# q and k of batches 2 to 7 transposed by DMA two batches ahead, those of batches 0 and 1 on the matrix engine

## The chip, the core and the metric

The kernel runs on one core of one Trainium2 chip. A core has five engines that each run their own list of instructions: PE (matrix multiply, with its weight loads shown apart as PEld), ACT (ScalarE), DVE (VectorE), POOL (GpSimd) and SP (SyncE). Here POOL issues all loads, and SP issues the stores of the output. Sixteen DMA engines carry what both issue. The metric is the device time of one execution in microseconds (us), lower is better.

## The reference

Eight batches of causal attention with a window of 128 and an ALiBi slope, eight heads of 64, 576 positions; the result is laid out as 4608 tokens of 512 and goes through two matrix products with h * cos(h) between them.

```python
scores = scale * np.matmul(q, k.transpose(0, 1, 3, 2))
bias = slopes[:, None, None] * (-np.abs(rel).astype(np.float32))[None, :, :]
mask = (rel >= 0) & (rel < window)
scores = np.where(mask, scores + bias[None], -1000000000.0)
attn = softmax(scores)                       # over the keys
attn_out = np.matmul(attn, v)
x = attn_out.transpose(0, 2, 1, 3).reshape(4608, 512)
h = x @ w_in                                 # 512 x 2048
out = (h * np.cos(h)) @ w_out                # 2048 x 512
```

Inputs and output are float32 in memory; the kernel computes in bf16 and accumulates in float32.

## The kernel before

Work is cut in two ways: attention goes by **batch** (8 of 576 tokens), the two matrix products go by **chunk** (9 of 512 tokens). The main loop runs over chunks c: `moe1(c)` (first product, line 596; for chunk 0 in halves, line 619; then the cosine on ACT, line 601, and the product on DVE, line 605), then `attention(c + 1)`, then `moe2(c)` (second product, line 642, whose result is copied to `ob` and stored by SP, line 654).

For the scores, q and k of a batch must lie with the head's 64 dimensions on the partitions. Before, `load_qk` (line 298) brings q and k into `qrows` and `krows` with the sequence on the partitions: eight DMAs per batch, issued by POOL. `qk_transposes` (line 375) then turns them over on PE. One call is a group of 18 transposes into two PSUM banks, followed by two copies (lines 386 on ACT, 387 on DVE, whichever is free) into `qt` and `kt`. A batch has four such calls (q and k, two halves each): 72 transposes and 8 copies. `qt` and `kt` exist once; `qrows` and `krows` too. In the loop they belong to batch c + 1 and stand between the moe1 matmuls of chunk c or in the last part of the attention before it.

Attention works in units of two heads and 256 queries, and a ninth unit for the last 64 queries of all heads ("t"). Each unit is a chain over engines: scores on PE (lines 414 and 424), exp on ACT (446, 454), mask on DVE (462, 469), probabilities times v on PE (490, 492, 504, 507), division on DVE (524 to 538), transposing back on PE (554, 568), and a copy into `xT` (582 on ACT, 583 on DVE).

PSUM has eight banks: `SB` 4 to 7 for scores, `UB` 2 and 3 for the attention output, `OB` 0 and 1 for moe2; moe1 borrows from UB and SB, and the q and k transposes from SB.

The order on each engine is written by a list scheduler inside the kernel (`Plan.schedule`): every operation has a planned occupation and latency and a priority, and the engine that can start first gets its best candidate. The result is a fixed list per engine. At run time an engine only waits on semaphores; if something is late, all that stands behind it on its engine waits too. POOL and SP kept program order before the change.

Of the kernel before, what the change touches and what calls it, by code (L numbers as in the profile page):

```python
# [13 lines left out]
NBLK = 5  # L14
# [20 lines left out]
class Plan:  # L35
# [3 lines left out]
    SWITCH = 95  # L39
    TABLE = 1330  # L40

    def __init__(self, nc, ctx):
# [44 lines left out]
    def schedule(self):  # L87
        free = {e: 0 for e in ENG}
        wire = 0
        mode, table = 0, None  # L90
# [18 lines left out]
        while avail:  # L109
# [130 lines left out]
def bass_alibi_sliding__then__act_gcu_kernel(  # L240
# [8 lines left out]
    with ExitStack() as ctx:  # L249
# [30 lines left out]

        ps = ctx.enter_context(nc.psum_tensor("ps", [128, 8, 512], F32))
        SB, UB, OB = [4, 5, 6, 7], [2, 3], [0, 1]

        slopes = [2.0 ** (-8.0 * (h + 1) / H) for h in range(H)]

        def keys_ap(x, pr, c):
            t = tr["k"][:, :].rearrange("p (k t) -> p k t", k=NPAIR)
            return t[64 * x:64 * x + 64, pr, 128 * c:128 * c + 128]

        def query_ap(x, pr, blk, width):  # L290
            t = tr["q"][:, :].rearrange("p (k t) -> p k t", k=NPAIR)
            return t[64 * x:64 * x + 64, pr, 128 * blk:128 * blk + width]


        def load_qk(which, src, b, pl):
            fns = []
            for g in range(2):
# [3 lines left out]
                        "h (s j) d -> s h (j d)", j=9)))  # L301
            op("pool", fns, w=[("qB", which, pl)], dma=f"ld{which}{pl}", occ=1250, lat=1250)

        def load_v(b, order=range(NBLK)):
            for t in order:
# [20 lines left out]
        def constants():  # L326
# [19 lines left out]
            op("dve", lambda e: e.memset(halfpi[:, :], math.pi / 2.0), w=["halfpi"])  # L346
            op("dve", lambda e: e.memset(
                tr["k"][:, :].rearrange("p (k t) -> p k t", k=NPAIR)[:, :, 576:640], 0.0),
               w=["ktail"])

# [12 lines left out]

        def qk_transposes(which, pl, banks):
            jj = ((0, 5), (5, 9))
# [15 lines left out]
            for n, (j0, j1) in enumerate(jj):  # L381
                o = tr[which][:, :].rearrange("p (g l t) -> p g l t", g=2, l=2)[
                    :, :, pl, 0:576].rearrange("p g (s j) -> p g s j", j=9)[:, :, :, j0:j1]
# [3 lines left out]
                    "dve": lambda e, o=o, i=i: e.tensor_copy(o, i)},  # L387
                   w=[("B", banks[n]), ("tr", which, pl, j0)],
# [3 lines left out]
        def tkeys(pr=None):  # L392
            pls = range(2) if pr is None else [pr % 2]
            return [("tr", w_, pl, j0) for w_ in ("q", "k") for pl in pls for j0 in (0, 5)] + [
                "ktail"]

# [6 lines left out]
        def scores(b, us):  # L403

            def f(e):
                ins = None
                for u, n in us:
                    banks = SB[2 * (n % 2):2 * (n % 2) + 2]
                    if u[0] == "t":
                        for pr in range(NPAIR):  # L410
                            for half in range(2):
                                for x in range(2):
                                    c0 = 128 * pr + 64 * half
                                    ins = e.matmul(ps[:, banks[x], c0:c0 + 64],
                                                   keys_ap(x, pr, 3 + half),
                                                   query_ap(x, pr, 4, 64), start=True, stop=True)
                        continue
# [4 lines left out]
                    for (c0, c1, kc, qb, nb) in jobs:  # L422
                        for x in range(2):
                            ins = e.matmul(ps[:, banks[x], c0:c1], keys_ap(x, pr, kc),  # L424
                                           query_ap(x, pr, qb, 128 * nb), start=True, stop=True)
                return ins
            keys, held, occ = [], [], 0
            for u, n in us:
                keys += tkeys(None if u[0] == "t" else u[0])
                held += [("B", x) for x in SB[2 * (n % 2):2 * (n % 2) + 2]]  # L430
# [248 lines left out]
        for pl in range(2):  # L679
            for i, which in enumerate(("q", "k")):  # L680
                qk_transposes(which, pl, (UB, OB)[i])
        for u in range(4):
# [64 lines left out]
```

## Time and profile before

| | |
|---|---|
| median of 3 runs | 348.78 us (348.36 to 348.86) |
| the profiled execution | 348.81 us, of which the profile's span is 346.8 us |
| PE busy | 331.8 us (96%) |
| ACT busy | 235.7 us (68%) |
| DVE busy | 203.9 us (59%) |
| POOL busy | 79.6 us (23%) |
| q and k transposes on PE | 576, of 2976 matmul instructions |
| loads (software queue) | 50944 packets, 18.36 MB |
| stores (hardware queue) | 5184 packets, 9.44 MB |

The span is the time from the first to the last event of the profile; the 2.0 us that the execution takes beyond it lie outside. An instruction's duration on PE runs from its start to its modelled end, and the next one starts long before that end, so that what an instruction costs on PE is read from the distance of starts, not from durations.

### The profile page before, as it was taken

The page shows a single profiled execution, that of the slowest core. Times are in us where ns is not written, and L with a number is a line of the kernel's source. Part 1 is how long each engine was busy: PE and PEld are TensorE (multiplying, and loading weights), DVE is VectorE, ACT ScalarE, POOL GpSimd, SP SyncE. Part 2 cuts the span into 40 slices and gives each one's busy share as a digit, 9 for nine tenths or more (in the row PEclk, how much of TensorE's full clock was granted, in tenths as well). Part 3 has the DMA queues.
Part 4 walks back from the last instruction along what each step waited for, and adds up shares of the span by engine and source line. Part 5 has one row for each costly group of instructions (what it writes and reads, how often), then busy time and mean ns, then how long its engine had stood idle before and what let it go on. Part 6 is the DMA issues. An engine that isn't in the chain of part 4 may idle for free.

```text
span 346.8 us, 7278 instructions
## 1 busy us (share of the span) xinstructions
PE 331.8 (96%) x2976; PEld 172.4 (50%) x2976; DVE 203.9 (59%) x452; ACT 235.7 (68%) x346; POOL 79.6 (23%) x121
## 2 busy tenths in 40 slices
PE   2689999999999999999999999999999999999996
PEld 1468746445644554455445544554445444444442
DVE  2479759677767768783858557673568344064000
ACT  3878859886688798787787876786686655164121
POOL 8992631160206021502430216000000000000000
PEclk9999999999999999999999999999999999999999
DMA  6999999496329453904491419100010000100212
GB/s 94 159 207 204 196 200 111 66 108 93 69 31 145 54 91 46 132 32 70 82 117 53 80 39 130 61 32 30 2 63 33 29 2 32 61 30 31 92 60 91
DMA packets 56160, 28.25 MB, mean 81 GB/s; under 512 B 39232, under 2 KB 51520, under 8 KB 56128
## 3 DMA queue, kind: packets, MB, share of 16 engines
q0 software_dynamic: 50944, 18.36, 47.3%
q1 hardware_dynamic: 5184, 9.44, 7.3%
q8 instruction: 23, 0.38, 0.4%
q14 instruction: 9, 0.07, 0.1%
HBM read 36.70 MB, written 9.44 MB: 133 GB/s over the span
## 4 chain that ended last, share of the span: by engine, by line
PE 90%; ACT 4%; POOL 2%; DMA 1%; DVE 1%; issue 1%; POOLq 0%; ACTq 0%
PE ps L642 34%; PE ps L596 33%; PE ps L375 5%; PE ps L424 5%; PE ps L619 3%; PE ps L504 3%; PE ps L568 2%; PE ps L507 2%; DMA krows<-in_k_dram 1%; ACT ptail L446 1%; ACT L446 1%; PE ps L490 1%; POOL qrows L298 1%; DVE ptail L462 1%; ACT p L454 1%
## 5 line engine op out<-in xcount | busy, mean ns | idle before, releaser
L642 PE MATMUL ps<-w_outb,gT 128*128 128x512 bf16 x576 | 139.0, 379 | 0.0
L605 DVE TENSOR_TENSOR gT<-ps,cos 128x512 bf16<-128x512 f32 x128 | 81.5, 686 | 70.0 <-PE ps L642 53.7
L596 PE MATMUL ps<-xT,w_inb 128*128 128x512 bf16 x512 | 121.0, 380 | 0.0
L601 ACT ACTIVATE cos<-ps,halfpi 128x512 f32<-128x512 f32 x128 | 82.4, 688 | 25.9 <-PE ps L642 13.4
L642 PEld LDWEIGHTS ps<-w_outb,gT 128*128 128x128 bf16 x576 | 53.7, 98 | 57.9 <-issue 2.2
L596 PEld LDWEIGHTS ps<-xT,w_inb 128*128 128x128 bf16 x512 | 46.1, 98 | 56.1 <-DVE gT L605 7.1
L454 ACT ACTIVATE p<-ps 128x768 bf16<-128x768 f32 (+1 forms) x64 | 56.2, 916 | 19.4 <-PE ps L424 19.3
L298 POOL DMA_DIRECT2D qrows<-in_q_dram x32 | 19.7, 632 | 122.4 <-PE ps L375 60.7
L648 ACT ACTIVATE ob<-ps 128x512 f32<-128x512 f32 x31 | 18.5, 596 | 42.5 <-PE ps L642 42.4
L469 DVE TENSOR_TENSOR p<-p,emask 128x768 bf16<-128x768 bf16 (+1 forms) x64 | 39.4, 615 | 2.5 <-ACT p L454 2.3
L307 POOL DMA_DIRECT2D vp<-in_v_dram x40 | 34.1, 908 | 0.0
L538 DVE TENSOR_TENSOR xnat<-ps,rec 128x256 bf16<-128x256 f32 x64 | 26.6, 418 | 0.5
L504 PE MATMUL ps<-vp,p 128*128 128x65 bf16 x256 | 22.8, 198 | 1.8 <-DVE p L469 1.5
L424 PE MATMUL ps<-qt,kt 64*128 64x128 bf16 (+1 forms) x320 | 20.6, 253 | 1.9 <-ACT kt L386 1.9
L504 PEld LDWEIGHTS ps<-vp,p 128*128 128x128 bf16 x256 | 17.0, 100 | 10.8 <-DVE xT L583 3.2
L298 POOL DMA_DIRECT2D krows<-in_k_dram x32 | 19.5, 633 | 10.9 <-PE ps L596 7.5
L507 PE MATMUL ps<-vp,p 128*128 128x65 bf16 x192 | 20.4, 196 | 0.0
L375 PE MATMUL ps<-ident,qrows 128*64 128x128 bf16 x288 | 12.0, 233 | 6.6 <-DMA qrows<-in_q_dram 6.6
L568 PE MATMUL ps<-ident,xnat 128*128 128x128 bf16 x128 | 18.1, 224 | 0.1
L582 ACT ACTIVATE xT<-ps 128x256 bf16<-128x256 bf16 (+3 forms) x34 | 11.9, 353 | 8.2 <-PE ps L568 8.1
L386 ACT ACTIVATE kt<-ps 128x640 bf16<-128x640 bf16 (+1 forms) x20 | 15.0, 780 | 3.5 <-PE ps L375 3.2
L386 ACT ACTIVATE qt<-ps 128x512 bf16<-128x512 bf16 (+1 forms) x21 | 15.3, 756 | 2.7 <-PE ps L375 2.3
(49 smaller groups left out, 245.7 us busy)
## 6 DMA issues: line engine op xcount, KB each, us to landing
out_dram<-ob SPq DMA_DIRECT2D x36, 256.0 KB, 2.0
qrows<-in_q_dram POOLq DMA_DIRECT2D x32, 144.0 KB, 3.2
krows<-in_k_dram POOLq DMA_DIRECT2D x32, 144.0 KB, 4.3
vp<-in_v_dram POOLq DMA_DIRECT2D x32, 128.0 KB, 4.7
w_inb<-in_moe_w_in_dram POOLq DMA_DIRECT2D x4, 512.0 KB, 9.8
w_outb<-in_moe_w_out_dram POOLq DMA_DIRECT2D x4, 512.0 KB, 18.2
vp<-in_v_dram POOLq DMA_DIRECT2D x8, 64.0 KB, 4.2
```

Of the source, the lines that this page charges most:

```text
L298: fns.append(lambda e, g=g: e.dma_start(qB[which][64 * g:64 * g + 64, 2 * pl:2 * pl + 2, :], src[b, 4 * g + 2 * pl:4 * g + 2 * pl + 2, :, ...
L307: op("pool", [lambda e, t=t, rows=rows: e.dma_start(vp[b % 2][0:rows, t, :, 0:64], v[b, :, 128 * t:128 * t + rows, :].rearrange("h p d -> ...
L375: ins = e.transpose(dst(n)[64 * x:64 * x + 64, 128 * (j - j0):128 * (j - j0) + 128], qB[which][:, 2 * pl + x, 64 * j:64 * j + 64], ident[: ...
L386: {"act": lambda e, o=o, i=i: e.activation(o, i, ACTF.Copy), "dve": lambda e, o=o, i=i: e.tensor_copy(o, i)},
L424: ins = e.matmul(ps[:, banks[x], c0:c1], keys_ap(x, pr, kc), query_ap(x, pr, qb, 128 * nb), start=True, stop=True)
L454: op("act", lambda e: e.activation(P[i][:, :, lo:512], src_[:, :, lo:512], ACTF.Exp, scale=0.125), w=held + [("P", i)], occ=920 if u[1] el ...
L469: op("dve", lambda e: e.tensor_tensor(P[i][:, :, lo:512], P[i][:, :, lo:512], EM[:, 2 * pr:2 * pr + 2, lo:512], ALU.mult), r=[("P", i), (" ...
L504: ins = e.matmul(o, P[i][:, x, d0:d0 + 128], V[:, kc, h, 0:65], start=True, stop=not two)
L596: op("pe", lambda e, kc=kc: e.matmul(ps[:, bank, :], w_in[:, kc, 128 * fc:128 * fc + 128], xT[:, kc, r0:r0 + CH], start=(kc == 0), stop=(k ...
L601: op("act", lambda e: e.activation(cosb[ci][:, :], ps[:, bank, :], ACTF.Sin, bias=halfpi[:, 0:1]), r=["halfpi"], w=[("B", bank), ("cos", c ...
L605: op("dve", lambda e: e.tensor_tensor(gT[gi][:, fc, :], ps[:, bank, :], cosb[ci][:, :], ALU.mult), r=[("cos", ci)], w=[("B", bank), ("g", ...
L642: op("pe", lambda e, t=t, fc=fc, bank=bank: e.matmul(ps[:, bank, :], gT[gi][:, fc, 128 * t:128 * t + 128], w_out[:, fc, :], start=(fc == 0 ...
```

## The change

Batches 0 and 1 stay as they were. For batches 2 to 7, `load_nat` brings q and k into new tiles `qnat` and `knat` with positions on the partitions and all heads side by side: five DMAs per tensor, of the same shapes as the five that load v. `dma_transposes` then has SP issue two DMA transposes per tensor (four 128-row blocks in one, the last 64 rows in the other), which write `qt` and `kt` directly. `qt` and `kt` exist twice now, by batch parity; `qnat` and `knat` once. The columns of `kt` beyond position 576 are cleared by `tail_zero` for batches 2 and 3, since the layout of the two kinds differs. SP no longer keeps program order: the scheduler places its operations. The scheduler's model of DMA is altered in three places, and moe1 goes round the six banks of UB and SB.

```diff
@@ Plan
+    WIRE0 = 4600
-        if eng in ("pool", "sp"):
+        if eng == "pool":
...
-        wire = 0
+        wire = self.WIRE0
...
-                wire = max(wire, st + o.occ + 1400) + o.lat
-                o.end = wire + 500
+                wire = max(wire, st + 2300) + o.lat
+                o.end = max(wire, st + o.occ + 1400) + 500
@@ tiles
-        tr = {"q": sb("qt", [128, 2560]), "k": sb("kt", [128, 2560])}
+        nat = {"q": sb("qnat", [128, NBLK, H, D]), "k": sb("knat", [128, NBLK, H, D])}
+        tr = {w_: [sb(f"{w_}t{i}", [128, 2560]) for i in range(2)] for w_ in ("q", "k")}
...
+        def keys_ap(b, x, pr, c):
+            lo, t = slice(64 * x, 64 * x + 64), tr["k"][b % 2][:, :]
+            if b < BPE:
+                return t.rearrange("p (k t) -> p k t", k=NPAIR)[lo, pr, 128 * c:128 * c + 128]
+            return t.rearrange("p (c k t) -> p c k t", c=NBLK, k=NPAIR)[lo, c, pr, :]
...
+        def load_nat(which, src, b):
+            fns = []
+            for t in range(NBLK):
+                rows = 128 if t < 4 else 64
+                fns.append(lambda e, t=t, rows=rows: e.dma_start(
+                    nat[which][0:rows, t, :, :],
+                    src[b, :, 128 * t:128 * t + rows, :].rearrange("h p d -> p h d")))
+            op("pool", fns, w=[("nat", which)], dma=f"ldn{which}", occ=4400, lat=4000)
+
+        def dma_transposes(b):
+            for which in ("q", "k"):
+                t = tr[which][b % 2][:, :].rearrange("p (c k t) -> p c k t", c=NBLK, k=NPAIR)
+                fns = [
+                    lambda e, t=t, which=which: e.dma_start_transpose(
+                        t[:, 0:4, :, :].rearrange("p c k t -> p (c k) t"),
+                        nat[which][:, 0:4, :, :].rearrange("p c h d -> p (c h d)")),
+                    lambda e, t=t, which=which: e.dma_start_transpose(
+                        t[:, 4, :, 0:64],
+                        nat[which][0:64, 4, :, :].rearrange("p h d -> p (h d)")),
+                ]
+                op("sp", fns, r=[("nat", which)] + ([("ktail", b % 2)] if which == "k" else []),
+                   w=[("tr", which, b % 2)], dma=f"tr{which}{b % 2}", occ=2500, lat=4400)
...
@@ main loop, inside "if c < B - 1"
                 if c == 0:
...
                     for pl in range(2):
-                        qk_transposes("q", pl, SB[2:4])
-                        qk_transposes("k", pl, SB[2:4])
+                        qk_transposes(1, "q", pl, SB[2:4])
+                        qk_transposes(1, "k", pl, SB[2:4])
+                    load_nat("q", q, 2)
+                    load_nat("k", k, 2)
+                    load_v(2, (3, 4, 0, 1, 2))
                 else:
-                    qk_transposes("q", 0, SB[0:2])
-                    qk_transposes("k", 0, SB[2:4])
                     for fc in range(NFC):
-                        if fc == 8:
-                            qk_transposes("q", 1, SB[0:2])
-                        if fc == 12:
-                            qk_transposes("k", 1, SB[0:2])
-                        moe1(c, fc, (UB + SB + UB + SB[2:] + UB + SB[2:] + UB)[fc])
+                        moe1(c, fc, (UB + SB)[fc % 6])
+                attention(c + 1)
                 if c + 2 < B:
-                    for pl in range(2):
-                        load_qk("q", q, c + 2, pl)
-                        load_qk("k", k, c + 2, pl)
-                    load_v(c + 2, (3, 4, 0, 1, 2))
-                attention(c + 1)
+                    if c < 2:
+                        tail_zero(c + 2)
+                    dma_transposes(c + 2)
+                if c + 3 < B:
+                    load_nat("q", q, c + 3)
+                    load_nat("k", k, c + 3)
+                    load_v(c + 3, (3, 4, 0, 1, 2))
```

What this does to the order shows at three places. Line numbers shift: after the change line 642 is moe1 (596 before), 688 is moe2 (642 before), 460 and 470 are the scores (414 and 424), 614 the transposing back (568), 536 and 538 the last unit's product with v (490 and 492).

PE, from the middle of moe1 of chunk 2 to the ninth unit of attention of batch 3. Before:

```order
L642 MATMUL ps<-w_outb,gT 128x512 x9
L596 MATMUL ps<-xT,w_inb 128x512 x8
L642 MATMUL ps<-w_outb,gT 128x512
L375 MATMUL ps<-ident,qrows 64x128 x18
L596 MATMUL ps<-xT,w_inb 128x512 x11
L375 MATMUL ps<-ident,krows 64x128 x18
L596 MATMUL ps<-xT,w_inb 128x512 x21
L414 MATMUL ps<-qt,kt 128x64 x16
L424 MATMUL ps<-qt,kt 128x256 x2
L424 MATMUL ps<-qt,kt 128x128 x2
L642 MATMUL ps<-w_outb,gT 128x512 x15
L490 MATMUL ps<-vp,ptail 128x65
```

After the change:

```order
L688 MATMUL ps<-w_outb,gT 128x512 x9
L642 MATMUL ps<-xT,w_inb 128x512 x40
L688 MATMUL ps<-w_outb,gT 128x512 x10
L460 MATMUL ps<-qt,kt 128x64 x16
L470 MATMUL ps<-qt,kt 128x256 x2
L470 MATMUL ps<-qt,kt 128x128 x2
L688 MATMUL ps<-w_outb,gT 128x512 x15
L536 MATMUL ps<-vp,ptail 128x65
```

The forty matmuls of moe1 now stand in one piece, without the two groups of transposes, and ten matmuls of moe2 have moved between the last of moe1 and the first scores.

PE, the end of attention of batch 2, where the other two groups of the next batch stood. Before:

```order
L424 MATMUL ps<-qt,kt 128x128 x4
L375 MATMUL ps<-ident,krows 64x128 x18
L642 MATMUL ps<-w_outb,gT 128x512
L568 MATMUL ps<-ident,xnat 128x128 x2
L642 MATMUL ps<-w_outb,gT 128x512
L375 MATMUL ps<-ident,qrows 64x128 x18
L642 MATMUL ps<-w_outb,gT 128x512
L568 MATMUL ps<-ident,xnat 128x128 x2
```

After the change:

```order
L470 MATMUL ps<-qt,kt 128x128 x4
L614 MATMUL ps<-ident,xnat 128x128 x2
L642 MATMUL ps<-xT,w_inb 128x512 x2
L688 MATMUL ps<-w_outb,gT 128x512 x3
L614 MATMUL ps<-ident,xnat 128x128 x2
L642 MATMUL ps<-xT,w_inb 128x512
```

Between the steps of the attention chain there are now matmuls of moe1 and moe2 alone; moe1 of the next chunk begins earlier.

SP, its first rows. Before it had one row, the 36 stores. After the change (`out_dram<-ob` is a store, `qt<-qnat` and `kt<-knat` are the transposes of batches 2, 3 and so on):

```order
L700 DMA out_dram<-ob 128x512 x2
L339 DMA_TRANSPOSE qt<-qnat 128x16x128
L342 DMA_TRANSPOSE qt<-qnat 128x4x64
L339 DMA_TRANSPOSE kt<-knat 128x16x128
L342 DMA_TRANSPOSE kt<-knat 128x4x64
L700 DMA out_dram<-ob 128x512
L339 DMA_TRANSPOSE qt<-qnat 128x16x128
L342 DMA_TRANSPOSE qt<-qnat 128x4x64
L700 DMA out_dram<-ob 128x512
L339 DMA_TRANSPOSE kt<-knat 128x16x128
L342 DMA_TRANSPOSE kt<-knat 128x4x64
L700 DMA out_dram<-ob 128x512 x2
```

So the third store stands behind the transposes of batch 2, the fourth and fifth behind those of batch 3, and a transpose that waits for its load holds up the stores behind it. On POOL, the ten loads of `qnat` and `knat` for batch 2 follow directly on the v loads of batch 1; those of a later batch come before its v and wait until the transposes of the batch before have read `qnat` and `knat`.

More of the change, by code (lines that the diff above doesn't have):

```diff
@@ L301, in load_qk @@
                         "h (s j) d -> s h (j d)", j=9)))
-            op("pool", fns, w=[("qB", which, pl)], dma=f"ld{which}{pl}", occ=1250, lat=1250)
+            op("pool", fns, w=[("qB", which, pl)], dma=f"ld{which}{pl}", occ=1250, lat=1450)
         def load_v(b, order=range(NBLK)):
@@ L346, in constants, with tail_zero @@
             op("dve", lambda e: e.memset(halfpi[:, :], math.pi / 2.0), w=["halfpi"])
+            for i in range(2):
+                op("dve", lambda e, i=i: e.memset(
+                    tr["k"][i][:, :].rearrange("p (k t) -> p k t", k=NPAIR)[:, :, 576:640], 0.0),
+                   w=[("ktail", i)])
+        def tail_zero(b):
             op("dve", lambda e: e.memset(
-                tr["k"][:, :].rearrange("p (k t) -> p k t", k=NPAIR)[:, :, 576:640], 0.0),
-               w=["ktail"])
+                tr["k"][b % 2][:, :].rearrange("p (c k t) -> p c k t", c=NBLK, k=NPAIR)[
+                    :, 4, :, 64:128], 0.0), w=[("tr", "k", b % 2), ("ktail", b % 2)], occ=250,
+               lat=300)
         def masks():
@@ L361, in masks, with qk_transposes @@
                    r=[("EM", h) for h in range(x, H, 2)], w=["EMt"], occ=500, lat=580)
-        def qk_transposes(which, pl, banks):
+        def qk_transposes(b, which, pl, banks):
             jj = ((0, 5), (5, 9))
@@ L387, in qk_transposes, with tkeys @@
                     "dve": lambda e, o=o, i=i: e.tensor_copy(o, i)},
-                   w=[("B", banks[n]), ("tr", which, pl, j0)],
+                   w=[("B", banks[n]), ("tr", which, b % 2, pl, j0)],
                    occ={"act": (730, 620)[n], "dve": (750, 620)[n]},
                    lat={"act": (840, 735)[n], "dve": (815, 690)[n]}, pri=4)
-        def tkeys(pr=None):
+        def tkeys(b, pr=None):
+            if b >= BPE:
+                return [("tr", w_, b % 2) for w_ in ("q", "k")] + [("ktail", b % 2)]
             pls = range(2) if pr is None else [pr % 2]
-            return [("tr", w_, pl, j0) for w_ in ("q", "k") for pl in pls for j0 in (0, 5)] + [
-                "ktail"]
+            return [("tr", w_, b % 2, pl, j0) for w_ in ("q", "k") for pl in pls
+                    for j0 in (0, 5)] + [("ktail", b % 2)]
         def units(b):
@@ L414, in f @@
                                     ins = e.matmul(ps[:, banks[x], c0:c0 + 64],
-                                                   keys_ap(x, pr, 3 + half),
-                                                   query_ap(x, pr, 4, 64), start=True, stop=True)
+                                                   keys_ap(b, x, pr, 3 + half),
+                                                   query_ap(b, x, pr, 4, 64), start=True, stop=True)
                         continue
@@ L423, in f @@
                         for x in range(2):
-                            ins = e.matmul(ps[:, banks[x], c0:c1], keys_ap(x, pr, kc),
-                                           query_ap(x, pr, qb, 128 * nb), start=True, stop=True)
+                            ins = e.matmul(ps[:, banks[x], c0:c1], keys_ap(b, x, pr, kc),
+                                           query_ap(b, x, pr, qb, 128 * nb), start=True, stop=True)
                 return ins
@@ L680, in bass_alibi_sliding__then__act_gcu_kernel @@
             for i, which in enumerate(("q", "k")):
-                qk_transposes(which, pl, (UB, OB)[i])
+                qk_transposes(0, which, pl, (UB, OB)[i])
         for u in range(4):
```

20 lines of the change are left out of this document (12 added, 8 removed).

## The prediction

> **What bounds the kernel now.** I read the page first (busy shares, slices, chain), then stretches by time, then PE's list around the groups that go.
>
> ```profile
> span 346.8 us, 7278 instructions
> PE 331.8 (96%) x2976; PEld 172.4 (50%) x2976; DVE 203.9 (59%) x452; ACT 235.7 (68%) x346; POOL 79.6 (23%) x121
> PE   2689999999999999999999999999999999999996
> PE 90%; ACT 4%; POOL 2%; DMA 1%; DVE 1%; issue 1%; POOLq 0%; ACTq 0%
> ```
>
> PE is busy in every slice from the fourth to the last but one, and 90% of the chain that ends last runs over it. But a busy PE could still be a PE that waits inside overlapping durations. The stretches, one per batch, show that no other engine is full:
>
> ```profile
> 57.00:89.00 32.00, 31.83 (x335) 16.42 (x333) 24.57 (x54) 25.76 (x37) 8.99 (x13) 1.00 0.60 75
> 191.00:228.00 37.00, 37.00 (x353) 18.78 (x352) 23.38 (x53) 27.77 (x43) 9.00 (x13) 1.00 0.53 70
> ```
>
> (Columns: window, its length, busy us and count of PE, PEld, DVE, ACT, POOL, then the granted clock, DMA share, GB/s.) ACT has 27.8 of 37 us, DVE 23.4, POOL 9; the clock is granted in full. And the starts of PE's instructions show how tightly they stand:
>
> ```profile
> 65.50 1.89 PE L596 MATMUL ps<-xT,w_inb 128*128 128x512 bf16 x8
> 67.22 0.38 PE L642 MATMUL ps<-w_outb,gT 128*128 128x512 bf16 x1
> 67.53 0.69 PE L375 MATMUL ps<-ident,qrows 128*64 128x128 bf16 x18
> 68.16 2.55 PE L596 MATMUL ps<-xT,w_inb 128*128 128x512 bf16 x11
> 70.64 0.69 PE L375 MATMUL ps<-ident,krows 128*64 128x128 bf16 x18
> 71.26 1.04 PE L596 MATMUL ps<-xT,w_inb 128*128 128x512 bf16 x4
> 227.95 0.38 PE L642 MATMUL ps<-w_outb,gT 128*128 128x512 bf16 x1
> 228.26 0.69 PE L375 MATMUL ps<-ident,krows 128*64 128x128 bf16 x18
> 228.89 0.20 PE L504 MATMUL ps<-vp,p 128*128 128x65 bf16 x1
> ```
>
> Eight 512-wide matmuls start within 67.22 - 65.50 = 1.72 us, 0.215 us each, with nothing between. So PE is bound by its own work from about 20 us to the end, and what is taken off it shortens the run, as long as what remains still finds its data ready.
>
> **What the change removes from PE.** From the start of the lone moe2 matmul at 67.22 to the first matmul behind the group (68.16) is 0.94 us; without the group it would be 0.215. The group costs 0.725 us: 0.63 for its 18 transposes, and 0.31 - 0.215 = 0.095 to change over into them. The others agree: 70.64 to 71.26 is 0.62, and the eleven matmuls before it take 2.48 instead of 2.37, together 0.73; in the attention phase 228.26 to 228.89 is 0.63, plus 0.31 - 0.215, again 0.725.
>
> ```profile
> L375 PE MATMUL ps<-ident,qrows x288: 219/219/316, 6.6 to 242.6; 128*64 128x128 bf16 x144
> L375 PE MATMUL ps<-ident,krows x288: 219/219/316, 8.1 to 244.6; 128*64 128x128 bf16 x144
> ```
>
> 576 transposes are 32 groups of 18, four per batch; six batches of eight lose theirs, 24 groups. **First term: 24 x 0.72 = 17.3 us.**
>
> The Trainium skill, "TensorE: Matmul & The Clock Gate", Part 4: PE-mode transpose, puts one 128 x 128 transpose at about 275 ns in one kernel's context, and by that price 432 of them would be 119 us and the time near 230. The rows above have a duration of 219 ns for each, and yet 18 within 0.63 us, since they overlap; the measured distance decides, and I give that result a chance of 0.01.
>
> **Smaller things on PE.** The last unit's product with v now and then waits for the mask:
>
> ```profile
> 142.89 3.41 PE L642 MATMUL ps<-w_outb,gT 128*128 128x512 bf16 x15
> 146.47 0.19 PE L490 MATMUL ps<-vp,ptail 128*128 128x65 bf16 x1 [0.17 <-DVE ptail L462]
> PE ps L490 <- DVE ptail L462: 0.5, 3, 0.2
> 10.99 1.17 PE L375 MATMUL ps<-ident,qrows 128*64 128x128 bf16 x18
> ```
>
> Fifteen matmuls need 15 x 0.215 = 3.23 us, the next starts 3.58 after the first: 0.35 lost, three times. The new order has eight or more moe2 matmuls (1.7 us) ahead of the scores there, which covers it: 1.0 us gained. And a return from moe2 to moe1 sometimes waits for a bank, in the chain of waits:
>
> ```profile
> 65.66 1.73 PE ps L596 x8
> 165.39 1.89 PE ps L596 x8
> ```
>
> The same eight cost 0.16 more at 165 us. In the order before, moe1 and moe2 alternate there several times per batch, around the transposes that hold SB banks; now forty moe1 matmuls stand in one piece. Two or so of these per batch in three batches: up to 1.0 us; with 0 as the other end I take 0.8. Against that, the start is written anew: q's second half is turned before the first scores, which may then come up to 1.8 us later (a group at the start, 1.17 us at 10.99, and its wait), while the masks that ACT made later are made earlier; the bounds are -1 to +1, I take -0.3. **Second term: 1.0 + 0.8 - 0.3 = 1.5 us.**
>
> **What ACT and DVE lose.** Three quarters of these copies go:
>
> ```profile
> L386 ACT ACTIVATE qt<-ps x21: 723/762/836, 7.8 to 243.1; 128x512 bf16<-128x512 bf16 x12, 128x640 bf16<-128x640 bf16 x9
> L386 ACT ACTIVATE kt<-ps x20: 732/770/837, 9.3 to 244.9; 128x640 bf16<-128x640 bf16 x14, 128x512 bf16<-128x512 bf16 x6
> L387 DVE COPY kt<-ps x12: 696/731/825, 9.3 to 244.9; 128x512 bf16<-128x512 bf16 x10, 128x640 bf16<-128x640 bf16 x2
> ```
>
> 48 copies of some 0.76 us, 36 us over two engines. I count them as nothing: PE set the pace. They are the reserve that keeps ACT and DVE from becoming the bound when a batch shrinks from 37 to about 34 us (ACT 27.8 - 4 = 24 of 34, the same share as now). The three added memsets on DVE (under 0.3 us each) stand in DVE's idle time.
>
> **What is added lies off the path, if it is in time.** Each batch gets ten loads of v's form in place of eight of 144 KB:
>
> ```profile
> L307 POOL DMA_DIRECT2D vp<-in_v_dram x40 | 34.1, 908 | 0.0
> vp<-in_v_dram POOLq DMA_DIRECT2D x32, 128.0 KB, 4.7
> q0 software_dynamic: 4796, 0.70, 136.7%
> out_dram<-ob SPq DMA_DIRECT2D x36, 256.0 KB, 2.0
> 22.84 4.43 POOL L307 DMA_DIRECT2D vp<-in_v_dram  x5
> DMA to landing us min/median/max: 3.6/4.6/21.5
> 75.90 0.41 PE L414 MATMUL ps<-qt,kt 64*128 64x64 bf16 x16
> 88.36 0.33 PE ps L424 x6
> 142.38 0.41 PE L414 MATMUL ps<-qt,kt 64*128 64x64 bf16 x16
> ```
>
> POOL: 15 x 0.908 = 13.6 us per batch of 34, after 9. The rings: one v (4796 packets) went through within a window of 7.5 us, so three such tensors need at most 22.5 us per batch. Neither is full. A DMA transpose is nowhere in this trace. Call T the time for one tensor (590 KB in bf16, two DMAs). From below: by bytes at the store's pace (256 KB in 2.0 us) 4.6 us; from above: v's, in small pieces, 7.5 us on the rings and 4.6 to land, 12 us. I take 5, nearest to the store, which SP issues too.
>
> The Trainium skill, "DMA: Bandwidth & Descriptors", Latency and other measured facts, has 261 GB/s for a DMA transpose; an estimate by that figure is 590 KB / 261 GB/s = 2.3 us for a tensor, no run here shows it, and the sum would not change.
>
> When must it be done? Batch 2 is the tight one. The v loads of batch 1, issued up to 27.3 us, land by 27.3 + 21.5 = 48.8; qnat follows by 56.3 and knat by 63.8. Batch 2's first scores start at 75.9 now, about 73 when its own four groups are gone. Two transposes in a row from 56.3 on are in time up to **T = 8.3 us**. For later batches, the earliest start is the last score of the batch two before (attention 2: 88.4 + 0.3), the latest end the first score (attention 4: 142.4); less two batches' gain that is some 48 us for two tensors: T up to 24. At T = 12 only batch 2 is late, by 2 x 12 - 16.7 = 7 us; at T = 5 nothing is. SP's stores wait behind the transposes, but each `ob` is needed again only four stores, a whole batch's time, later.
>
> Full rings do not slow PE either:
>
> ```profile
> 43.00:57.00 14.00, 14.00 (x164) 7.41 (x164) 9.82 (x27) 9.92 (x13) 3.20 (x4) 1.00 1.71 190
> 44.99 3.34 PE ps L642 x15
> 179.22 3.34 PE ps L642 x15
> ```
>
> Fifteen matmuls take 3.34 us both at a DMA share of 1.71 and in a stretch of about 0.5.
>
> **The sum.** 17.3 + 1.5 = 18.8 us. The profiled execution's own time is 348.81 (span 346.8 and 2.0 around it, which stay), 0.03 from the median of the runs; 348.8 - 18.8 = **330.0 us**.
>
> **The rivals.**
> 1. *The groups in the attention phase were filling.* Two of a batch's four groups stand between steps of the exp-mask-product chain. If PE only waits there instead, 12 groups are worth nothing: 8.6 + 1.5 = 10.1 gained, **338.7**. For it: exps wait for scores and DVE is 63 to 77% busy (23.4 of 37 us, 24.6 of 32). Against: moe2 and the next moe1 fill those places in the new order, and ACT and DVE lose their copies at the same time. Chance 0.10.
> 2. *Batch 2 is late at the upper bound.* T = 12: 7 us lost once, **337**. Chance 0.04.
> 3. *Slower: the transposes are slow.* Past T = 24 each batch waits for its own, past T = 18 batch 2 alone eats the gain (2 x 18 - 16.7 = 19). At twice my upper bound, T = 24, batch 2 is late by 31 us, the rest just in time: 330 + 31 = **361**. Small pieces speak for it, the deep lead of two batches against. Chance 0.05.
> 4. *No change:* ACT and DVE with their table changes set the pace and PE's gain is idle time, **348.8**. Against it: ACT's 25% of idle time. Chance 0.02.
> That PE's groups do not go is ruled out by the order.
>
> **How the numbers follow.** 0.78 for the forecast, 0.10, 0.04, 0.05, 0.02, and 0.01 for the page's price. The likeliest case's own range is 328 to 333 (second term -0.5 to +3, 17.3 fixed). To reach 8 in 10 with the unknown T and some of rival 1, it goes from 327 to 338. Faster by over 0.2% (0.7 us, about what a measurement of this kernel tells from no change): 0.78 + 0.10 + 0.04 + 0.01 = 0.93; within it 0.02; slower 0.05.
>
> **What the changed profile would show.** Right: 144 matmuls at line 419, the last before 45 us; moe1 in pieces of 40 whose starts stand 0.215 apart; batches of 31 to 34 us; both scores lines never waiting for DMA; DMA transposes landing in under 8 us. Rival 1: waits of PE for DVE's mask or ACT's exp of over 0.3 us, several per batch. Rivals 2 and 3: PE waiting at lines 460 or 470 for a DMA into `kt` at 73 us, or in every batch. I would be wrong if PE's busy time falls by 17 us and the span by much less.

## The result and the profile after

The changed kernel takes 329.65 us (median of 4 runs, 329.22 to 330.08) against 348.57 us: a ratio of 0.9457, 95% interval 0.9438 to 0.9476. That is 18.9 us less, where 18.8 was forecast. The profiled execution took 330.08 us.

The page of the kernel after, busy shares, PE's and DMA's slices, and the shares of the chain that ended last:

```profile
span 328.4 us, 6317 instructions
PE 311.0 (95%) x2504; PEld 161.5 (49%) x2544; DVE 197.9 (60%) x440; ACT 212.6 (65%) x313; POOL 101.3 (31%) x133
PE   2589999999999999999999999999999999999995
DMA  6999999999999999991999395100010000201112
PE 89%; DVE 3%; ACT 2%; POOL 2%; issue 2%; DMA 1%; POOLq 0%; ACTq 0%
```

PE is still the bound, with 20.8 us less by the page; ACT has 23 us less and DVE 6. (Some matmul records are missing here: 2504 of 2544, by the count of weight loads. A gap of 0.43 us between two 512-wide matmuls in the trace is such a hole. The page counts 3.1 us of idle time before lines 688 and 642, where the kernel before has 0.0, so up to 3 of the 20.8 us are holes of this kind.)

Where did the time come from? The stretches from one batch's first ninth-unit score to the next, before and after (columns: window, length, busy us and count of PE, PEld, DVE, ACT, POOL, then clock, DMA share, GB/s). Before:

```profile
44.40:75.90 31.50, 31.50 (x323) 16.37 (x324) 22.59 (x51) 24.87 (x36) 9.29 (x15) 1.00 0.95 120
75.90:110.30 34.40, 34.23 (x336) 17.58 (x336) 25.82 (x57) 26.24 (x40) 9.11 (x14) 1.00 0.61 84
178.60:216.00 37.40, 37.40 (x351) 18.71 (x352) 23.68 (x54) 28.22 (x44) 9.00 (x13) 1.00 0.55 77
253.30:346.80 93.50, 90.19 (x531) 41.30 (x530) 32.43 (x67) 41.45 (x64) 0.00 (x0) 1.00 0.13 49
```

After:

```profile
45.00:76.30 31.30, 31.01 (x260) 15.32 (x265) 22.24 (x49) 23.58 (x36) 13.56 (x17) 1.00 1.80 160
76.30:109.80 33.50, 33.13 (x272) 16.84 (x278) 23.44 (x52) 24.18 (x37) 16.84 (x21) 1.00 1.87 166
173.00:204.70 31.70, 31.43 (x262) 15.94 (x267) 23.65 (x53) 22.86 (x36) 4.20 (x5) 1.00 0.78 92
237.10:328.40 91.30, 87.04 (x511) 40.37 (x520) 31.75 (x66) 40.02 (x62) 0.00 (x0) 1.00 0.13 50
```

The first two batches became hardly shorter, though each lost four groups. In the first stretch PE had 324 weight loads before and 265 after: 59 fewer, not 72, so 13 matmuls of moe2 have moved into the place of the groups. Their time comes back later: the stretch at 179 us went from 37.4 to 31.7, and the last one lost 2.2. The gain of a group is paid out where the moved work would have stood.

The added work. The queues of the kernel after (packets, MB, share of 16 engines' span), and the issues (count, median us from issue to landing):

```profile
q0 software_dynamic: 100288, 18.36, 70.7%
q1 hardware_dynamic: 33600, 16.52, 21.9%
qt<-qnat SPq DMA_TRANSPOSE x12, 4.4
kt<-knat SPq DMA_TRANSPOSE x12, 6.5
```

In SP's list each DMA transpose holds SP for the time in the second column:

```profile
54.87 5.40 SPq L339 DMA_TRANSPOSE qt<-qnat  x1
60.31 1.24 SPq L342 DMA_TRANSPOSE qt<-qnat  x1
61.60 2.70 SPq L339 DMA_TRANSPOSE kt<-knat  x1
64.34 1.81 SPq L342 DMA_TRANSPOSE kt<-knat  x1
```

Twice as many packets in the software queue, and the rings are full up to the eighteenth slice. Batch 2's transposes begin at 54.9 us and its scores at 76.3. PE's waits after the start name no DMA into `kt` or `qt`:

```profile
PE ps L419 <- POOL ident L375: 6.0, 1, 6.0
PE ps L550 <- DVE p L515: 1.6, 2, 1.5
PE ps L419 <- DMA qrows<-in_q_dram: 1.2, 1, 1.2
PE ps L419 <- DMA krows<-in_k_dram: 0.9, 1, 0.9
```

### The profile page after: what moved, and what is told of

Same layout as the page of the kernel before. It is cut to its first block, busy times and chain, and to the rows that moved or that the text cites. A ratio compares the mean times of both kernels' runs of the same rounds, so it can differ in the third digit from the quotient of the medians.

```text
span 328.4 us, 6317 instructions
## 1 busy us (share of the span) xinstructions
PE 311.0 (95%) x2504; PEld 161.5 (49%) x2544; DVE 197.9 (60%) x440; ACT 212.6 (65%) x313; POOL 101.3 (31%) x133
## 4 chain that ended last, share of the span: by engine, by line
PE 89%; DVE 3%; ACT 2%; POOL 2%; issue 2%; DMA 1%; POOLq 0%; ACTq 0%
PE ps L688 37%; PE ps L642 33%; PE ps L665 5%; PE ps L470 5%; PE ps L550 3%; PE ps L614 2%; PE ps L553 2%; DMA krows<-in_k_dram 1%; PE ps L419 1%; DVE p L515 1%; ACT p L500 1%; PE ps L460 1%; POOL qrows L311 1%; PE ps L536 1%; PE ps L538 1%
## 5 line engine op out<-in xcount | busy, mean ns | idle before, releaser
L688 PE MATMUL ps<-w_outb,gT 128*128 128x512 bf16 x548 | 133.4, 379 | 1.9 <-issue 0.6
L642 PE MATMUL ps<-xT,w_inb 128*128 128x512 bf16 x500 | 117.9, 379 | 1.2 <-DVE gT L651 0.4
L642 PEld LDWEIGHTS ps<-xT,w_inb 128*128 128x128 bf16 x512 | 46.8, 98 | 55.8 <-DVE gT L651 4.8
L694 ACT ACTIVATE ob<-ps 128x512 f32<-128x512 f32 x24 | 14.3, 597 | 33.8 <-PE ps L688 33.8
L330 POOL DMA_DIRECT2D qnat<-in_q_dram x30 | 25.5, 920 | 30.9 <-DMA qt<-qnat 30.9
L330 POOL DMA_DIRECT2D knat<-in_k_dram x30 | 25.6, 926 | 5.4 <-DMA kt<-knat 5.0
L628 ACT ACTIVATE xT<-ps 128x256 bf16<-128x256 bf16 (+3 forms) x41 | 14.5, 355 | 18.0 <-PE ps L614 17.9
L696 DVE COPY ob<-ps 128x512 f32<-128x512 f32 x12 | 8.3, 690 | 18.4 <-PE ps L688 18.0
L582 DVE RECIPROCAL rec<-ps 128x4 f32<-128x4 f32 x64 | 11.5, 180 | 11.5 <-PE ps L553 10.4
L665 PE MATMUL ps<-xT,w_inb 128*128 128x256 bf16 x128 | 17.4, 281 | 0.7 <-ACT ptail L492 0.5
```

The lines of the kernel that those rows point to most:

```text
L330: fns.append(lambda e, t=t, rows=rows: e.dma_start(nat[which][0:rows, t, :, :], src[b, :, 128 * t:128 * t + rows, :].rearrange("h p d -> p ...
L642: op("pe", lambda e, kc=kc: e.matmul(ps[:, bank, :], w_in[:, kc, 128 * fc:128 * fc + 128], xT[:, kc, r0:r0 + CH], start=(kc == 0), stop=(k ...
L665: op("pe", lambda e, i=i, fc=fc, kc=kc: e.matmul(ps[:, bank, 256 * i:256 * i + 256], w_in[:, kc, 128 * fc:128 * fc + 128], xT[:, kc, r0:r0 ...
L688: op("pe", lambda e, t=t, fc=fc, bank=bank: e.matmul(ps[:, bank, :], gT[gi][:, fc, 128 * t:128 * t + 128], w_out[:, fc, :], start=(fc == 0 ...
```

## The experiments

The theory: PE is full, so each group of 18 transposes that leaves it is worth its 0.72 us wherever it stood, and the DMA side costs nothing while it is in time. The rivals: the groups in the attention phase filled waits; the relief of ACT and DVE, or the new order, brought the gain; the DMA side is tight.

| kernel | median, us | ratio to before | 95% interval |
|---|---|---|---|
| groups in the attention phase cut, old order | 347.79 | 0.9960 | 0.9945 to 0.9975 |
| groups among moe1 cut, old order | 345.17 | 0.9887 | 0.9871 to 0.9904 |
| copies shrunk, old order | 349.35 | 0.9999 | 0.9988 to 1.0010 |
| planner and banks alone | 346.82 | 0.9930 | 0.9915 to 0.9945 |
| that, without the attention-phase groups | 338.89 | 0.9709 | 0.9693 to 0.9725 |
| that, without the groups among moe1 | 338.93 | 0.9705 | 0.9689 to 0.9722 |
| that, without all 24 groups, no DMA transposes | 330.16 | 0.9458 | 0.9441 to 0.9475 |
| the change | 329.65 | 0.9457 | 0.9438 to 0.9476 |
| the change, first DMA time 0 | 329.79 | 0.9453 | 0.9436 to 0.9470 |
| the change, transposes twice | 334.88 | 0.9596 | 0.9565 to 0.9628 |
| the change, transposes three times | 370.07 | 1.0621 | 1.0601 to 1.0641 |
| the change, transposes four times | 432.56 | 1.2387 | 1.2362 to 1.2412 |
| the change, batch 1 by DMA too | 340.15 | 0.9757 | 0.9737 to 0.9777 |

The kernel before took 348.6 to 349.3 us in these comparisons; differences below are worked out from the ratios, of 348.8 us.

### Groups cut short, the order kept

```diff
                         for x in range(2):
+                            if cut and j > j0:
+                                continue
                             ins = e.transpose(
...
                 i = dst(n).rearrange("p (j g s) -> p g s j", j=j1 - j0, g=2)
+                if cut:
+                    i = i[:, :, :, 0:1].broadcast_to([128, 2, 64, j1 - j0])
...
-                    qk_transposes("q", 0, SB[0:2])
-                    qk_transposes("k", 0, SB[2:4])
+                    qk_transposes("q", 0, SB[0:2], True)
+                    qk_transposes("k", 0, SB[2:4], True)
```

The second kernel has the flag at the other two calls. The groups of the first call stand in the attention phase, those of the second among the matmuls of moe1.

> The kernel before with the order of every engine unchanged, but of each group of 18 transposes that stands in the attention phase (12 groups, batches 2 to 7) only 4 are left; the copies stay as long and read those four again, so that half of q and k of these batches is not computed. Within a group the starts of 18 transposes span 474 ns; of four, some 58. Theory (PE is full, each start counts): 12 x 0.416 = 5.0 us less, 343.6 us. Rival (these groups only fill waits of the softmax chain): nothing, 347.5 or more.

> The same cut for the 12 groups that stand among the matmuls of moe1; the order is that of the kernel before, the other half of q and k of batches 2 to 7 is not computed. Theory and rival both: 5.0 us less, 343.6 us. If the two runs differ, the place of a group counts.

Measured: 1.4 us less for the attention phase, 3.9 for moe1. In the trace of the second, PE's list around one group:

```profile
101.48 0.30 PE L377 MATMUL ps<-ident,qrows 128*64 128x128 bf16 x4
101.71 2.55 PE L600 MATMUL ps<-xT,w_inb 128*128 128x512 bf16 x11
```

From the group's start to the next matmul it takes 0.23 us instead of 0.63, so 0.40 each, 4.8 for twelve, of which 3.9 reached the end. In the attention phase the same cut ran into a wait. The kernel before, and then the cut one, at the end of attention 2:

```profile
88.89 0.42 DVE L538 TENSOR_TENSOR xnat<-ps,rec 128x256 bf16<-128x256 f32 x1
89.25 0.39 PE L642 MATMUL ps<-w_outb,gT 128*128 128x512 bf16 x1
89.48 0.28 PE L568 MATMUL ps<-ident,xnat 128*128 128x128 bf16 x2
```

```profile
89.19 0.39 PE L646 MATMUL ps<-w_outb,gT 128*128 128x512 bf16 x1
89.22 0.42 DVE L542 TENSOR_TENSOR xnat<-ps,rec 128x256 bf16<-128x256 f32 x1
89.68 0.11 PEld L572 LDWEIGHTS ps<-ident,xnat 128*128 128x128 bf16 x2 [0.40 <-DVE xnat L542]
```

Before, transposing back (line 568) starts 0.23 us behind the moe2 matmul ahead of it; with the group cut it starts 0.50 behind (89.69 by PE's own row), because the division on DVE (line 542) isn't done before 89.64. The same shows in every batch: from its first group in the attention phase to its first group among moe1, the cut kernel gains 0.15 to 0.37 us of the 0.80 that two cut groups save. So **in the old order the rival is mostly right**: of some 4.8 us in the attention phase 1.4 were real, the rest covered waits for the softmax chain. If that also held for the new order, the change would have gained about 12 us, not 19 (an estimate: 8.6 for the other groups, 1.4 to 2.5 for these, 1.5 to 2.4 for the second term).

### The copies on ACT and DVE

```diff
                 i = dst(n).rearrange("p (j g s) -> p g s j", j=j1 - j0, g=2)
+                if cut:
+                    o, i = o[:, 0:1, 0:8, :], i[:, 0:1, 0:8, :]
```

> The kernel before in its own order, all transposes on PE, but the 48 copies of batches 2 to 7 on ACT and DVE shrunk to an eighth of a half's rows each (most of q and k is not brought to qt and kt). Theory (ACT and DVE are not the bound): 0 to 0.5 us less, 348.1 to 348.6. Rival (part of the gain comes from these engines' relief): 1 us less or more, 347.5 or below.

No difference: ratio 0.9999. (The kept part is smaller than the expectation says, one sixteenth of a copy: one of two groups, 8 of 64 rows.) In the old order the relief of ACT and DVE alone is worth nothing.

### Planner and banks alone, then without the groups

```diff
+    WIRE0 = 4600
...
-        if eng in ("pool", "sp"):
+        if eng == "pool":
...
-                        moe1(c, fc, (UB + SB + UB + SB[2:] + UB + SB[2:] + UB)[fc])
+                        moe1(c, fc, (UB + SB)[fc % 6])
```

> The kernel before with only the altered DMA model of the scheduler, SP placed by it, and moe1 round the six banks of UB and SB; q and k stay on PE for all batches. Theory: banks give up to 1.0 us, the start costs 0.3 to 0.5: 347.5 to 349.5. Rival (the new order, not the missing groups, brings the gain): below 343.

(The two altered lines of the DMA model are left out here. So is a planned latency of `load_qk`, 1450 for 1250 ns, which this kernel and the change both have and which the description of the change doesn't name.)

2.4 us less, more than the theory's 1.3 and far from the rival's 6. The rest of the gain must come from the groups. Since the cut groups had shown that this depends on the order, the next three kernels start from this one and take groups out before planning:

```diff
-                    qk_transposes("q", 0, SB[0:2])
-                    qk_transposes("k", 0, SB[2:4])
                     for fc in range(NFC):
...
-                        if fc == 8:
-                            qk_transposes("q", 1, SB[0:2])
-                        if fc == 12:
-                            qk_transposes("k", 1, SB[0:2])
```

(the first two lines in one, the other four in the next, all six in the third).

> The fourth kernel (planner and banks alone, 346.8 us) without the 12 groups of batches 2 to 7, and their copies, that stood in the attention phase in the first run: half of q and k of these batches is not turned over, the scores read what batch 1 left; order planned anew, no DMA transposes. Theory (with a fixed order these groups cover waits for the softmax chain, but a new order puts moe matmuls there that have to be done anyway): 12 x 0.72 = 8.6 us less, 338.2. Rival (the waits stay whatever the order): 2 us less or little more, 344 to 345.

> The same without the other 12 groups, those among the matmuls of moe1. Theory and rival both: 8.6 us less, 338.2.

> The same without all 24 groups and without any DMA transpose: q and k of batches 2 to 7 are loaded but never turned over, so that the scores are those of batch 1's q and k. Theory (the DMA side of the change costs PE nothing): 24 x 0.72 = 17.3 less than 346.8, 329.5, the same as the changed kernel's 329.65 within 0.7. Rival (loads and transposes cost something hidden): 328.5 or below.

7.7, 7.8 and 16.5 us less than planner and banks alone. The two kinds of groups are worth the same and add up within the intervals (15.5 beside 16.5), 0.64 to 0.69 us a group. So once the order is made anew, taking out the attention-phase groups saves nearly their whole time. PE's two rows of waits for DVE in attention are the same with these groups (planner and banks alone) and without them: 2.2 us for the mask and 0.5 us for the division. The copies on ACT and DVE went with the groups in these three kernels; what they bring alone in the new order was not measured. And the kernel without groups and without any DMA transpose is as fast as the change (0.9458 against 0.9457, each within some 0.6 us): natural loads, transposes, POOL's and SP's added work and twice the packets cost PE nothing that can be measured.

### How late the transposes may be

```diff
-                op("sp", fns, r=[("nat", which)] + ([("ktail", b % 2)] if which == "k" else []),
-                   w=[("tr", which, b % 2)], dma=f"tr{which}{b % 2}", occ=2500, lat=4400)
+                for n in range(2):
+                    op("sp", fns, r=[("nat", which)] + ([("ktail", b % 2)] if which == "k" else []),
+                       w=[("tr", which, b % 2)], dma=f"tr{which}{b % 2}",
+                       occ=0 if n else 2500, lat=-1 if n else 4400)
...
+            if o.lat < 0:
+                o.end = st
+            elif o.dma is not None:
```

The repeats cost the planner nothing, so that PE, ACT, DVE and POOL keep their order; each waits for the one before on the same tensor. They do not stand in a row, though: SP's list has for a batch q, k, then the other passes of q, then the other passes of k.

> The changed kernel with the order of PE, ACT, DVE and POOL unchanged, but each tensor's DMA transposes done twice in a row on SP, the second after the first has landed: T doubles. In the profile after the change batch 2's q goes from 54.9 to 64.2 and its k lands at 68.7; its first scores are at 76.3. Theory (batch 2 is the tight one): k lands near 80 to 84, PE waits 4 to 8 us once, 334 to 338 us, later batches in time. Rival (more slack than that): 329.7. Rival (every batch is tight): over 345.

> The same with each tensor's transposes done four times, T some 19 to 26 us, the order of the computing engines unchanged. By the prediction's bound (later batches bear T up to 24) only batch 2 is late, by 21 to 33 us: 351 to 363 us. Rival (SP works off both tensors of a batch one after the other, so that 2T must fit in a batch's 32 us; T up to 16): batch 2 late by some 30, each of the five later batches by another 6 to 15: 390 to 430 us.

Twice: 5.2 us more. Four times: 103 more, 2.6 us above the rival's range. PE's waits at the scores, with two and with four passes (us in total, times, longest):

```profile
PE ps L464 <- DMA kt<-knat: 3.7, 1, 3.7
```

```profile
PE ps L464 <- DMA kt<-knat: 90.9, 6, 23.8
```

With two, batch 2 alone is late, by 3.7 us, as the theory had it. With four, all six are, the first by 23.8, and from then on the scores of successive batches start at 99.3, 147.2 and 195.0 us: 48 us for a batch. That speaks for the rival: the transposes need more than a batch's time in every batch. A run with three passes was to tell a limit of 16 us for T from one of 24:

> Each tensor's DMA transposes three times, the order of PE, ACT, DVE and POOL that of the changed kernel. With four passes batch 2 was 24 us late and a batch took 48 us, with two it was 3.8 us late and later batches were in time: a pass of one tensor takes some 48 / 8 = 6.0 us in a row, T is 18 here. Theory (SP turns both tensors of a batch over one after the other, 2T = 36 us, more than the 32 us of a batch): batch 2 late by 14, the five later ones by about 4 each: 355 to 364 us. Rival (the prediction's bound, T up to 24 for later batches): only batch 2 late, 341 to 346 us.

```profile
PE ps L464 <- DMA kt<-knat: 30.3, 6, 13.4
```

All six batches late again: with T at some 18 us the lead of two batches isn't enough here, against the bound of 24 us. The first is late by 13.4, as expected; the time is above the range, 370 for 355 to 364. The waits for DMA make up 30.3 of the 40.4 us that it is slower than the change; the rest is in the last section.

A batch took 38 to 39 us here, not 36, and the chain of waits shows what fills it (start, length, what). Behind the last pass of batch 2's k, which lands at 88.0:

```profile
88.30 3.46 POOL knat L332 x4
91.77 5.66 DMA knat<-in_k_dram
97.44 1.32 SPq L341
```

`knat` exists once. It is loaded again only when the last pass has read it, and until then the next batch's k can't begin; SP issues no transpose from 90.6 to 97.4 us. The reload takes 9.0 us between batches 3 and 4, and five passes of 6.0 follow (135.0 to 164.9 us). With four passes it is 11.0 us (99.3 to 110.3) and then seven passes of 5.3, not eight of 6.0. So the two runs show a rate limit, the reload being a part of it. Where T's limit lies with one pass per tensor, where q's only pass can run during the reload of `knat`, they don't show.

### The start, and batch 1

```diff
-    WIRE0 = 4600
+    WIRE0 = 0
```

> The changed kernel with the scheduler's first DMA time set back to 0, which changes the order in the first 45 us alone for the most part. In the profiles attention of batch 1 starts at 44.9 us after the change and at 44.4 before. Theory (the new start costs 0.5 us): 329.2. Rival (the start is set by the loads of batch 0, whatever the order): 329.7, no difference to be told.

No difference (329.79 beside 329.65): the later start of attention 1 in the profile, 44.9 for 44.4, isn't due to this constant. It may be no effect at all: in the traces of the three kernels with the old order, attention 1 starts at 44.6, 44.7 and 45.0 us.

```diff
-        BPE = 2
+        BPE = 1
...
-        for pl in range(2):
-            load_qk("q", q, 1, pl)
-            load_qk("k", k, 1, pl)
+        load_nat("q", q, 1)
+        load_nat("k", k, 1)
+        tail_zero(1)
+        dma_transposes(1)
...
-            if c < 2:
+            if c < 1:
```

(and without the PE groups of batch 1).

> The changed kernel with batch 1 too by DMA: its ten loads in place of eight, and its transposes on SP before any store. Four more groups leave PE. If the transposes land in time: 2.9 us less, 326.8. Rival (the rings are full until 57 us, so that w_out, v and the transposes of batch 1 come late): 330 to 336, with PE waiting between 40 and 60 us.

10.5 us slower than the change. SP's list:

```profile
31.60 1.53 SPq L339 DMA_TRANSPOSE qt<-qnat  x1
41.32 8.75 SPq L339 DMA_TRANSPOSE kt<-knat  x1
50.11 1.25 SPq L342 DMA_TRANSPOSE kt<-knat  x1
```

And two pieces of the chain of waits (start, length, what):

```profile
25.74 23.09 DMA w_outb<-in_moe_w_out_dram
48.88 5.79 PE ps L688 x26
```

k of batch 1 is turned over only between 41 and 51 us, and w_out lands at 48.8 behind the natural loads. Attention 1, at 44.9 in the change, starts at 57.6. PE stands idle for 6.8 us between 44 and 64 us, and from 61.9 to 72.1 us the granted clock is at half (why, the last section shows), which by estimate takes another 4 to 5 us of PE's work. Removing four more groups from PE gains nothing where the rings are full and the lead is missing.

## Why the prediction was right, and where not

- **What bounds the kernel:** right. The transposes' own distance of starts (0.72 us a group), not their duration, gave the size. The Trainium skill's 275 ns for a transpose ("TensorE: Matmul & The Clock Gate", Part 4: PE-mode transpose) is no price for them here: the measured worth of 18 transposes with their change-over is 0.69 us, 38 ns each.
- **First term, 24 x 0.72 = 17.3:** measured 16.5, as what planner and banks alone leave to the change. But one half of it stood on a ground that the prediction only argued (rival 1, chance 0.10): in the old order the attention-phase groups do cover waits, and a wait appeared as soon as they shrank. In the new order they are worth nearly their full time (7.7 of 8.6 us), and the order shows moe1 and moe2 matmuls in their places, which have to be done anyway. "What is taken off it shortens the run" is true of PE's total, with enough work that can be moved, not of each place.
- **Second term, 1.5:** planner and banks alone gave 2.4. Of its parts, the wait of the last unit for the mask (1.0) is gone, with planner and banks alone as after the change: PE's waits have no row for it any more, and around 143 us the way from the first moe2 matmul to that product is 3.25 us instead of 3.58. That the start costs 0.3 isn't shown; attention 1 starts 0.5 later in the profile, no more than it varies among kernels with the same list. What the banks brought was not measured apart. The bounds given for the parts add up to 0 to 3.0, not to the -0.5 to 3 of the range. The errors of the two terms, -0.8 and +0.9, cancel: that the sum is right to 0.1 us is luck.
- **ACT and DVE at nothing:** right, 0.9999.
- **DMA side off the path:** right, the kernel without transposes is no faster. T was taken as 5 us, within 4.6 to 12; passes in the runs with repeats took 5.3 to 6.3, so 5 was somewhat low. Batch 2's q began at 54.9 and its k's last DMA was issued at 64.3, in time for 76.3. The median landings are 4.4 and 6.5 us per DMA.
- **Batch 2 the tight one:** right; with T doubled it alone was late, by 3.7 us.
- **"T up to 24" for later batches:** wrong: in two runs with T at 18 and at some 21 to 24 us every later batch was late. The step took the time between the last score of one batch and the first score two batches later, and halved it for two tensors. It left out that this work comes back with every batch, and that `qnat` and `knat`, which exist once, must be loaded again in between. By its own reckoning, two transposes in a row, 2T would have to fit in one batch's 32 us, so T up to 16; that figure is argued, not measured. The forecast didn't hang on it, but rival 3's price did: at T = 24 it had 361, and four passes gave 432.6.
- **Where the gain shows:** the prediction let batch 2's scores come 3 us earlier, at 73; they came at 76.3, no earlier than before, since 13 moved moe2 matmuls took the room. Batches of 31 to 34 us were right.

## What to carry to other kernels

Price an instruction that leaves a full engine by the distance of starts around it, change-over included, and ask then whether its place covered a wait: cutting the work with the order held fixed shows that (here 1.4 us of 4.8), and planning anew shows whether other work can move there (here nearly all). For a transfer that takes over such work there are two limits, the first deadline and the rate: all that comes back with every batch, the refilling of a buffer that exists once included, must fit in a batch's time. Check both, and leave on the engine what has no lead (batch 1 here cost 10.5 us).

## What the runs showed of the hardware that was not expected

A wait of PE can cost more than its length, since the granted clock falls in it or right behind it and stays down for some us. With four passes, around the end of the wait at 99.3 us (the third column from the end is the clock):

```profile
75.00:78.00 3.00, 0.49 (x3) 0.00 (x0) 0.29 (x1) 0.87 (x1) 0.00 (x0) 1.00 0.36 67
95.00:99.30 4.30, 0.03 (x2) 0.03 (x4) 0.00 (x0) 0.00 (x0) 0.00 (x0) 0.50 0.73 137
99.30:104.00 4.70, 4.37 (x29) 1.93 (x31) 1.51 (x3) 1.73 (x2) 4.49 (x6) 0.51 1.09 147
104.00:110.00 6.00, 5.95 (x73) 3.24 (x72) 3.52 (x12) 3.06 (x4) 3.88 (x5) 1.00 2.19 178
```

PE is busy again from 99.3 us on, but has half the clock for 4.7 us more. The ninth unit's scores, which stand right behind the wait, show it; the kernel after, and then four passes (ns least, median, most):

```profile
L460 PE MATMUL ps<-qt,kt x128: 186/190/200, 25.0 to 237.4; 64*128 64x64 bf16 x128
```

```profile
L464 PE MATMUL ps<-qt,kt x128: 186/238/238, 24.0 to 337.5; 64*128 64x64 bf16 x128
```

With three passes, the 8 us behind each of the six waits (13.4, 2.4, 5.0, 4.7, 3.5 and 1.3 us long):

```profile
88.00:96.00 8.00, 7.93 (x69) 3.72 (x69) 2.79 (x6) 2.69 (x4) 7.70 (x10) 0.73 1.49 166
126.00:134.00 8.00, 7.96 (x76) 3.84 (x77) 2.98 (x7) 3.10 (x4) 7.72 (x10) 0.79 1.63 153
164.90:172.90 8.00, 7.91 (x63) 3.65 (x64) 2.37 (x5) 1.88 (x3) 7.67 (x10) 0.63 1.52 165
203.40:211.40 8.00, 7.93 (x65) 3.70 (x65) 2.83 (x7) 2.37 (x3) 7.70 (x10) 0.69 1.51 193
241.10:249.10 8.00, 7.95 (x76) 3.85 (x77) 2.43 (x6) 3.66 (x5) 7.72 (x10) 0.79 1.50 190
276.60:284.60 8.00, 7.94 (x98) 4.25 (x99) 4.61 (x11) 4.22 (x6) 0.00 (x0) 1.00 0.44 164
```

What is missing from full clock there is 8 x (0.27 + 0.21 + 0.37 + 0.31 + 0.21) = 11.0 us of PE's work, about the 10.1 us by which three passes were slower than their waits. It is no function of a wait's length alone: 2.4 us of standing still cost clock here. With two passes, the stretch in which the wait of 3.7 us ends (at 79.8 us), and what follows:

```profile
79.00:87.00 8.00, 7.00 (x79) 3.69 (x83) 3.89 (x10) 3.77 (x5) 6.98 (x9) 1.00 1.29 125
```

The clock stays at 1.00 there. In the three other executions of this kernel the mean granted clock was 0.995, 0.994 and 0.98, and they took 334.3, 335.5 and 336.0 us beside 333.6 us: the same kernel loses clock in some executions and not in others.

The Trainium skill ("TensorE: Matmul & The Clock Gate", Part 1) has the array's clock halved after an idle window of some 3.4 us whose place is not tied to the kernel, and given back after about as long at work. The traces agree with such windows. With three passes the clock falls at 78.71, 126.49, 164.04, 201.59 and 242.55 us and comes back at 92.36, 129.91, 170.87, 208.42 and 245.96 us, read from the clock of stretches of half a us; all these times are whole multiples of 3.413 us apart (92.36 to 126.49 is ten of them). With four passes they are, too, from 80.04 us on. So the places do not follow the waits, and they differ between executions. Cut along these windows, the trace with three passes reads:

```profile
123.08:126.49 3.41, 1.02 (x23) 0.43 (x21) 0.28 (x1) 0.52 (x1) 0.21 (x1) 1.00 0.81 151
126.49:129.91 3.42, 3.42 (x12) 1.19 (x9) 0.09 (x1) 1.73 (x2) 3.42 (x5) 0.50 1.00 154
235.72:239.13 3.41, 1.91 (x9) 0.69 (x7) 1.38 (x2) 2.63 (x4) 0.00 (x0) 1.00 1.61 169
```

The wait of 2.4 us lies in one window, in which PE is busy for 1.02 of 3.41 us, and the clock is halved at its end, when PE is already at work again. A window need not be idle throughout: with three and four passes and with batch 1 by DMA, behind the first 25 us, each fall follows a window with at most 1.4 us of busy PE, and no fall follows a window with 1.9 us or more. That the 3.7 us with two passes were spared because two windows shared them is likely but not shown, as the clock of that trace never changes and so doesn't tell where its windows lie.
